# Tokens in rows of five and four: one row layout for q, k, v, the mixers and the output of a linear-attention and phase-mixing kernel

## The chip, the cores and the metric

The kernel runs on one core of a Trainium2 chip. The metric is the device time of one execution in microseconds (us), lower is better. "Before" ran in 232.32 us (median of 3 runs, 231.84 to 232.75). A profile is one further execution taken by the hardware profiler; its span is some 2 us shorter than the time. The engines are PE (matrix multiplication), PEld (its weight load), DVE (vector), ACT (scalar), POOL and SP. SP computes nothing here: it issues the DMA transfers. "SPq" in a profile is SP's sequencer, that is, the time in which SP is occupied with issuing.

## The reference, cut to what matters

```python
# q, k, v: (8 batches, 8 heads, 576 tokens, 64), float32
kv  = einsum('bhsd,bhse->bhde', k, v)
out = einsum('bhsd,bhde->bhse', q, kv)
x   = out / sqrt(mean(out*out, -1) + 1e-6) * g_norm      # -> (8, 576, 512)
theta = x @ w_theta
zr, zi = x * cos(theta), x * sin(theta)
y   = w_tok_r @ zr + w_tok_i @ zi        # "mixers": 576 x 576, over tokens
u   = x + y
return u + maximum(u @ w_ch, 0)
```

576 tokens are four and a half times the 128 rows (partitions) of the core's on-chip memory. The half is the subject of the change. Batches are independent, but theta needs all heads of a batch, and the mix needs all tokens of it.

## The kernel before: the parts that the change touches

A list scheduler in the kernel orders some thousand tasks by estimated times and then emits them; the order on every engine is fixed by it. A token layout puts tokens 0 to 511 into 128 rows of four, and the last 64 tokens ("tails") into tiles of their own:

```python
# load, per head pair: one transfer of 128 rows, two heads, 1 KB each (256 KB)
nc.sync.dma_start(
    out=t[:].rearrange("p h j d -> p h (j d)"),
    in_=src[b, pair, 0:SF, :].rearrange("h (p j) d -> p h (j d)", j=NF))
# batch 0 only, k and v: 128 rows of (head, token row), nine tokens each (288 KB)
    in_=src[b, pair].rearrange("h (p j) d -> (h p) (j d)", j=NS)
# tails, per batch and tensor: 64 rows x 8 heads x 256 B
nc.sync.dma_start(out=t[0:T], in_=src[b, :, SF:S, :].rearrange("h s d -> s h d"))
...
# mixer weights and output: 128 rows per transfer, the tails apart
chunk(name, w[0:SF, :].rearrange("(p j) s -> p j s", j=NF)[:, j, :] if j < NF else w[SF:S, :], ...)
nc.sync.dma_start(out=out[b, 0:SF, :].rearrange("(p j) c -> p j c", j=NF)[:, ti, :], in_=t[:])
for (half, r) in parts:                      # the output's tail: two transfers
    nc.sync.dma_start(out=out[b, SF:S, r * n:(r + 1) * n], in_=t[half])
```

The mixers are cast to fp16 by POOL alone. Batch 0 goes through the attention by head pair (a short chain), batch 1 and later by token tile. While PE has nothing else to do in the first 43 us it runs "warm" products whose results nobody reads.

## Time and profile before

| What | Value | Where read |
|---|---|---|
| time | 232.32 us | runs |
| PE busy, of it warm products | 220.8 us, 23.4 us | busy table, groups |
| first theta product | 25.19 us | timeline |
| batch 1's first theta, batch 1's first mix | 53.79, 68.44 us | timeline |
| from there to the last batch's last block of 63 mix products | 143.7 us, about 24 per batch | timeline |
| from there to the end of the span | 18.2 us | timeline |

These are lines of the page of the profile of before: the engines' busy time, two rows of tenths over 40 equal slices of the span (granted PE clock, DMA share), and the chain of waits that ended last.

```profile
PE 220.8 (96%) x2342; PEld 145.8 (63%) x2342; DVE 185.2 (80%) x368; ACT 157.3 (68%) x298; POOL 88.0 (38%) x108
...
PEclk9999999999999999999999999999999999999999
DMA  5899999999749996974899467996894412103214
...
PE 73%; DMA 9%; DVE 6%; ACT 5%; POOL 3%; issue 1%; SPq 1%; DVEq 0%
PE y L893 27%; PE vps L937 11%; PE th L806 11%; PE kv L524 6%; DMA wst<-in_moe_w_theta_dram 4%; PE xTps L775 4%; PE ups L928 4%; PE warm L293 3%; DMA vl<-in_v_dram 3%; PE raw L572 3%; DMA v<-in_v_dram 2%; POOL rt L594 2%; ACT tr L849 2%; DV
```

The chain is PE's, and SP's own share of it is 1%. DMA counts at the start, where the first batch comes in. PE busy at 96% overstates the bound, because the warm products are in it. The Trainium skill, "Trainium Kernel Development and Optimization", section "Performance Expectations", calls matmul busy time a bad measure for another reason, that matmuls are pipelined. That it misleads here through idle-filling products is this trace's own finding.

The stages of the batches show the bound better. This is a view by windows (columns: from, to and length in us, then busy us of PE, PEld, DVE, ACT, POOL with the number of instructions, granted PE clock, DMA share, GB/s). Two steady batches of before:

```profile
92.40:116.40 24.00, 23.80 (x267) 16.39 (x266) 22.14 (x45) 18.67 (x36) 10.46 (x10) 1.00 0.75 213
116.40:140.40 24.00, 24.00 (x266) 16.35 (x264) 21.53 (x45) 18.00 (x35) 9.94 (x10) 1.00 0.77 224
```

PE is busy in all but 0.2 us of the first window and in all of the second. And this is how SP issues the first loads: the timeline of SP in the first 3 us (start, duration, engine and line, what).

```profile
0.73 0.45 SPq L308 DMA_DIRECT2D q<-in_q_dram  x1
1.24 0.45 SPq L314 DMA_DIRECT2D k<-in_k_dram  x1
1.74 0.43 SPq L314 DMA_DIRECT2D v<-in_v_dram  x1
2.21 0.43 SPq L308 DMA_DIRECT2D q<-in_q_dram  x1
```

One 128-row transfer occupies SP for 0.43 to 0.45 us here.

### The profile page before, as it was taken

The page shows a single profiled execution, that of the slowest core. Times are in us where ns is not written, and L with a number is a line of the kernel's source. Part 1 is how long each engine was busy: PE and PEld are TensorE (multiplying, and loading weights), DVE is VectorE, ACT ScalarE, POOL GpSimd, SP SyncE. Part 2 cuts the span into 40 slices and gives each one's busy share as a digit, 9 for nine tenths or more (in the row PEclk, how much of TensorE's full clock was granted, in tenths as well). Part 3 has the DMA queues.
Part 4 walks back from the last instruction along what each step waited for, and adds up shares of the span by engine and source line. Part 5 has one row for each costly group of instructions (what it writes and reads, how often), then busy time and mean ns, then how long its engine had stood idle before and what let it go on. Part 6 is the DMA issues. An engine that isn't in the chain of part 4 may idle for free.

```text
span 230.3 us, 5955 instructions
## 1 busy us (share of the span) xinstructions
PE 220.8 (96%) x2342; PEld 145.8 (63%) x2342; DVE 185.2 (80%) x368; ACT 157.3 (68%) x298; POOL 88.0 (38%) x108
## 2 busy tenths in 40 slices
PE   7999999999996999999999999999999999999992
PEld 2674555786754665677667766865675668655861
DVE  2268599279997798799999997998799989987553
ACT  2477687327995688767896877589849797877031
POOL 8000197436513670464266033543275336430000
PEclk9999999999999999999999999999999999999999
DMA  5899999999749996974899467996894412103214
GB/s 184 291 344 239 291 254 313 330 272 335 127 124 260 340 162 159 331 235 82 190 317 353 90 151 213 318 195 155 234 306 122 117 57 93 48 23 137 71 46 159
DMA packets 59931, 46.42 MB, mean 202 GB/s; under 512 B 29056, under 2 KB 52608, under 8 KB 59904
## 3 DMA queue, kind: packets, MB, share of 16 engines
q1 hardware_dynamic: 59840, 46.05, 71.9%
q8 instruction: 18, 0.29, 0.6%
q14 instruction: 9, 0.07, 0.1%
q0 software_dynamic: 64, 0.00, 0.0%
HBM read 33.06 MB, written 9.44 MB: 185 GB/s over the span
## 4 chain that ended last, share of the span: by engine, by line
PE 73%; DMA 9%; DVE 6%; ACT 5%; POOL 3%; issue 1%; SPq 1%; DVEq 0%
PE y L893 27%; PE vps L937 11%; PE th L806 11%; PE kv L524 6%; DMA wst<-in_moe_w_theta_dram 4%; PE xTps L775 4%; PE ups L928 4%; PE warm L293 3%; DMA vl<-in_v_dram 3%; PE raw L572 3%; DMA v<-in_v_dram 2%; POOL rt L594 2%; ACT tr L849 2%; DVE x L606 2%; PE wTps L432 2%; PE th L811 1%
## 5 line engine op out<-in xcount | busy, mean ns | idle before, releaser
L893 PE MATMUL y<-wT,z 128*128 128x320 f16 (+1 forms) x576 | 79.1, 286 | 2.2 <-DVE z L859 2.2
L893 PEld LDWEIGHTS <-z 128*128 128x128 f16 x576 | 54.0, 98 | 19.1 <-DVE z L859 2.8
L594 POOL TENSOR_TENSOR rt<-ss,mhalf 128x8 f32<-128x8 f32 x35 | 61.0, 1744 | 2.9
L590 POOL TENSOR_SCALAR ss<-ss 128x8 f32<-128x8 f32 x35 | 9.5, 271 | 85.2 <-DVE ss L583 84.6
L901 DVE SCALAR_TENSOR_TENSOR uT<-y,gcol,xT 128x256 f16<-128x256 f32 (+1 forms) x64 | 32.7, 512 | 7.9 <-PE y L893 7.6
L937 PE MATMUL vps<-wch,uT 128*128 128x512 f16 (+1 forms) x192 | 37.7, 344 | 0.0
L818 ACT ACTIVATE pt<-th,magic_t 128x512 f32<-128x512 f32 (+1 forms) x40 | 25.7, 642 | 16.6 <-PE th L806 13.3
L806 PE MATMUL th<-wth,xT 128*128 128x512 f16 x128 | 32.7, 380 | 0.0
L784 ACT ACTIVATE xT<-xTps,gcol 128x512 f16<-128x512 f16 (+1 forms) x36 | 22.9, 635 | 13.3 <-PE xTps L775 13.0
L944 ACT COPY u<-ups 128x512 f16<-128x512 f16 (+1 forms) x40 | 21.0, 537 | 14.9 <-PE ups L928 14.6
L859 DVE TENSOR_TENSOR z<-x,tr 128x1024 f16<-128x1024 f16 (+1 forms) x40 | 27.0, 674 | 3.4 <-ACT tr L849 1.7
L948 DVE SCALAR_TENSOR_TENSOR ot<-vps,u 128x512 f32<-128x512 f32 (+1 forms) x40 | 25.2, 633 | 4.1 <-PE vps L937 2.6
L822 DVE SCALAR_TENSOR_TENSOR f<-pt,th 128x512 f32<-128x512 f32 (+1 forms) x40 | 25.2, 629 | 4.0 <-ACT pt L818 3.7
L606 DVE TENSOR_TENSOR x<-raw,rt 128x512 f16<-128x512 f32 x36 | 24.7, 685 | 3.0 <-POOL rt L594 2.4
L583 DVE TENSOR_REDUCE ss<-sq 128x8 f32<-128x512 f32 x36 | 24.3, 680 | 2.3 <-ACT sq L579 2.0
L293 PE MATMUL warm<-kvbd 128*128 128x512 f16 x81 | 23.4, 410 | 2.0 <-DVE pio_t L250 1.5
L841 ACT ACTIVATE tr<-fa,pio_t 128x512 f16<-128x512 f32 x32 | 23.0, 720 | 0.5 <-DVE fa L829 0.3
L841 ACT ACTIVATE tr<-f 128x512 f16<-128x512 f32 x32 | 20.2, 630 | 3.4 <-DVE f L822 3.2
L579 ACT ACTIVATE sq<-raw 128x512 f32<-128x512 f32 x36 | 21.1, 591 | 1.2 <-PE raw L572 0.9
L937 PEld LDWEIGHTS <-uT 128*128 128x128 f16 (+1 forms) x192 | 14.1, 102 | 8.1 <-issue 0.4
L524 PE MATMUL kv<-v,k 128*64 128x64 f32 x448 | 19.0, 227 | 0.0
L524 PEld LDWEIGHTS kv<-v,k 128*64 128x64 f32 x448 | 15.3, 137 | 5.6 <-issue 4.2
(80 smaller groups left out, 243.4 us busy)
## 6 DMA issues: line engine op xcount, KB each, us to landing
q<-in_q_dram SPq DMA_DIRECT2D x32, 256.0 KB, 5.1
out_dram<-ot SPq DMA_DIRECT2D x32, 256.0 KB, 3.6
k<-in_k_dram SPq DMA_DIRECT2D x28, 256.0 KB, 5.1
v<-in_v_dram SPq DMA_DIRECT2D x28, 256.0 KB, 5.5
k<-in_k_dram SPq DMA_DIRECT2D x4, 288.0 KB, 6.2
v<-in_v_dram SPq DMA_DIRECT2D x4, 288.0 KB, 6.4
wmix<-in_moe_w_tok_r_dram SPq DMA_DIRECT2D x4, 288.0 KB, 5.5
wmix<-in_moe_w_tok_i_dram SPq DMA_DIRECT2D x4, 288.0 KB, 4.0
```

Source lines behind the costliest of these rows:

```text
L293: nc.tensor.matmul(t[:], kv_bd[1][:, 0, :], kv_bd[1][:].rearrange("p h c -> p (h c)"), start=True, stop=True,)
L524: nc.tensor.matmul(kvp[r * D:(r + 1) * D, hp, :], st["k", b, hp][:, r, j, :] if j < NF else st["kl", b][:, 2 * hp + r, :], st["v", b, hp][ ...
L594: nc.gpsimd.tensor_tensor(out=r[:], in0=t[:], in1=mhalf[:], op=ALU.pow)
L606: nc.vector.tensor_tensor(out=t[:].rearrange("p (h e) -> p h e", h=H), in0=st[raw][:].rearrange("p (h e) -> p h e", h=H), in1=st[rt][:].un ...
L806: nc.tensor.matmul(t[:], xT[:, kc, :], wth[:, kc, :], start=(kc == 0), stop=(kc == NK - 1),)
L818: nc.scalar.activation(out=t[:], in_=st[th][:], func=AFT.Identity, bias=magic_t[:])
L822: nc.vector.scalar_tensor_tensor(out=t[:], in0=st[pt][:], scalar=MAGIC, in1=st[th][:], op0=ALU.subtract, op1=ALU.subtract,)
L841: nc.scalar.activation(out=t[:, which, :], in_=src[:], func=AFT.Sin, scale=-RAD, bias=0.0 if bias is None else bias[:],)
L859: nc.vector.tensor_tensor(out=t[:], in0=xb.unsqueeze(1).broadcast_to((P, w, C)), in1=st[tr][:, 0:w, :], op=ALU.mult,)
L893: nc.tensor.matmul(t[:], z[:, kc * P:(kc + 1) * P], wT[m][:, cols], start=(m == 0), stop=(m == NM - 1),)
L901: nc.vector.scalar_tensor_tensor(out=st["uT", b][:, kc, cols], in0=st[y][:], scalar=gcol[:], in1=st["xT", b][:, kc, cols], op0=ALU.mult, o ...
L937: nc.tensor.matmul(t[half], uT(kc), wch[:, kc, r * n:(r + 1) * n], start=(kc == 0), stop=(kc == NK - 1),)
```

## The change

Its intent: no separate tails (no tail loads, no tail casts, fewer products in batch 0), and a shorter start. The 576 tokens are laid in 128 rows of which 64 hold five tokens and 64 hold four: rows 0 to 63 take tokens 0 to 319, rows 64 to 127 tokens 320 to 575. The fifth slot of the lower rows is the tail. As five and four do not fit one regular access pattern, each load becomes two transfers of 64 rows; so do the mixers' loads and the stores. Besides, batch 1 goes by head pair like batch 0, the mixers are cast whole by whichever of POOL, DVE and ACT is free, they are loaded before batch 1, batch 0's mix adds up as its tiles arrive, the evictions of the first half of a mix merge two chunks, g_norm is brought into a column by a small product, and the scheduler's target times are new. The core of the diff:

```diff
-                    nc.sync.dma_start(
-                        out=t[:].rearrange("p h j d -> p h (j d)"),
-                        in_=src[b, pair, 0:SF, :].rearrange("h (p j) d -> p h (j d)", j=NF),
-                    )
+                for (rows, tokens, n) in ((slice(0, T), slice(0, L0), NT), (slice(T, P), slice(L0, S), NF)):
+                    nc.sync.dma_start(
+                        out=t[rows, :, 0:n, :].rearrange("p h j d -> p h (j d)"),
+                        in_=src[b, 2 * hp:2 * hp + 2, tokens, :].rearrange("h (p j) d -> p h (j d)", j=n),
+                    )
... (the tails' loads, casts and tiles go)
-                chunk(name, w[0:SF, :].rearrange("(p j) s -> p j s", j=NF)[:, j, :] if j < NF
-                      else w[SF:S, :], mixers + 0.1 + 0.1 * i + 0.01 * j)
+                parts = [(slice(0, T), lower(w)[:, j, :])]
+                if j < NF:
+                    parts.append((slice(T, P), upper(w)[:, j, :]))
+                chunk(name, parts, mixers + 0.1 + 0.1 * i + 0.01 * j)
-            weave.add(name, on[2:] if pool else on[:2], at, fn, needs=[of], uses=[of])
+            weave.add(name, [act(n), dve(0.06 + n / 1900.0, True), pool(n)], at, fn,
+                      needs=[of], uses=[of])
...
-                nc.sync.dma_start(
-                    out=out[b, 0:SF, :].rearrange("(p j) c -> p j c", j=NF)[:, ti, :], in_=t[:]
-                )
+                nc.sync.dma_start(out=lower(out[b])[:, ti, :], in_=t[0:T])
+                nc.sync.dma_start(out=upper(out[b])[:, ti, :], in_=t[T:P])
                 return
-            for (half, r) in parts:
-                nc.sync.dma_start(out=out[b, SF:S, r * n:(r + 1) * n], in_=t[half])
+            nc.sync.dma_start(
+                out=lower(out[b])[:, NF, :].rearrange("t (r c) -> r t c", r=len(parts)), in_=t[:]
+            )
+    SP2 = ("SP", 0.15, 0.15, False)     # the scheduler's cost of two transfers, us
```

## The prediction

> **What bounds the kernel.** TensorE. The page's busy table gives PE 220.8 of 230.3 us (96%), DVE 185.2, ACT 157.3; the chain of waits is 73% PE. But the groups by line show 81 idle-filling "warm" matmuls (23.4 us) in that PE time, so real PE work is about 197 us. By stage:
>
> - 0 to 25 us: PE waits. The timeline shows 51 warm matmuls (spaced 0.22 us, about 11 us) before the first theta product at 25.2 us. The chain there is DMA: v, w_theta (3.8% of the span), v tails (3.1%). Batch 0's last v is used at 16.1 us; the chain from there to turned x takes 8 us, then PE stands behind batch 1's k/v tails.
> - 25 to 68 us: mixed. 30 more warm matmuls (6.5 us), because the mixer weights are cast by POOL alone from 28.2 to 38.6 us; mix of batch 0 starts at 44.3, theta of batch 1 at 53.8, mix of batch 1 at 68.4 with PE idle 2.7 us in 60 to 80 us.
> - 68 to 212 us: PE saturated, 24.0 us per batch (six mix starts); a batch's PE groups sum to about 23.7.
> - 212 to 230 us: the last mix and channel product, 18 us.
>
> **What the change does.**
>
> 1. Tails as fifth slot: the 22 tail loads (512 packets of 256 B each, landing 4 us) and 8 tail casts (3.3 us DVE) go; batch 0's kv takes 10 instead of 18 slot pairs (about 0.85 instead of 1.2 us per pair of heads). Against it every q/k/v load is two DMAs of 64 rows, 24 issues of about 0.4 us for batch 0, and the instruction order shows that each DMA waits for the one eight before it, so half as many bytes are in flight. The Trainium skill, "SBUF — State Buffer", section "Door 1: The DMA port swizzle", says 64 adjacent rows reach half of the 16 ports; no run shows yet whether this bites.
> 2. Batch 1 goes by head pair: its theta follows its last pair by one short chain.
> 3. Mixers are cast whole by POOL, DVE and ACT, loaded before batch 1.
> 4. Batch 0's mix opens its sums as z tiles come; first-half mix evictions merge two chunks (DVE about 15 us falls to an estimated 10).
> 5. Mixer transposes double in number (45 to 90) but pair up on half the columns: estimated +1 us at most. Warm matmuls fall 81 to 39.
>
> **On the critical path.** What comes before mix of batch 1. Batch 0's 3.54 MB plus 1.05 MB at an estimated 325 GB/s land at about 14 and 17 us; with a 7 us chain theta starts near 21.5 us (gain 3.7). PE work from there to batch 1's theta sums to about 27 us, plus 9 warm: near 50 (gain 4). Mix of batch 1 near 63 instead of 68.4. The rest, 144 + 18 us, is PE-bound and equal: the evictions' saving on DVE is off the path.
>
> **Predicted: 225.0 us, 221.5 to 228.5 in 8 of 10.** Faster by over 2% 0.80, within 2% 0.18, slower 0.02.
>
> **What would show it.** First theta at 20 to 23 us; wT complete and batch 0's mix begun near 30; batch 1's theta at 47 to 51; mix starts 24 us apart after 63; last 18 us unchanged; warm time about 9 us; loads landing in 3 to 4 us at 300 GB/s or more.
>
> **What would make it wrong.** Half-port or half-depth loads falling under 280 GB/s early; ACT's order (a mixer cast ahead of batch 0's last turn) making theta wait for the mixers; new PE stalls from z or PSUM banks in the steady batches, so that the early gain is given back.

## The result

The changed kernel is correct and took 280.66 us (median of 4 runs, 279.3 to 282.49) against 232.38 us (median of 4, 231.84 to 232.75). The ratio is 1.2085, with a 95% interval of 1.2008 to 1.2162. Ratios here and below are the mean time of one kernel's fast runs over the mean of the other's fast runs of the same rounds, so not quite the ratio of the medians that are quoted. The predicted 225.0 us and its range were missed by far, in the wrong direction.

The same lines of the page, after, with PE's own row of busy tenths as well:

```profile
PE 230.3 (82%) x2283; PEld 152.7 (54%) x2283; DVE 184.5 (66%) x369; ACT 156.9 (56%) x299; POOL 76.7 (27%) x92
...
PE   7669929998798597697957799859967999999980
PEclk9876975999999799889997599979997999999998
DMA  5779868987767776777577666677466723403333
...
PE 36%; DMA 24%; SPq 20%; DVE 9%; issue 4%; POOL 2%; ACT 1%; POOLq 1%; DVEq 0%; ACTq 0%
PE y L864 13%; SPq L327 12%; DMA qin<-in_q_dram 12%; DMA out_dram<-ot 8%; PE vps L920 6%; PE kv L484 4%; PE th L768 4%; SPq L347 3%; SPq L467 3%; DVE x L554 2%; DMA wst<-in_moe_w_theta_dram 2%; DMA vin<-in_v_dram 2%; PE ups L911 2%; DVE ot 
```

DVE and ACT do as much as before. PE's share of the chain fell from 73% to 36%, and SP's sequencer went from 1% to 20%: L327 is the issue of the 64-row q, k and v. The DMA share is lower than before in 20 of the 40 slices and higher in 11, and over the span the hardware queue's packets took 64.2% in place of 71.9%: on the whole the DMA engines are not overloaded, they are waiting for work. The granted clock fell in places. The two rows above show its low digits (5 to 7) in slices where PE's own digit is 7 or less, or in the slice right after one (the 5 in the seventh slice follows PE's 2), so I take it as a companion of the waiting and use no slow-clock argument below. It is not free, though: PE was busy for 230.3 us here, and for 210.4 us with the same 2283 instructions in a2 below, at a clock of 0.916 against 0.991. How much of the loss passed through the clock no run separates.

SP in the timeline of after, at the start and where w_theta, the mixers and batch 1 are issued (x2 is two transfers):

```profile
0.73 1.44 SPq L327 DMA_DIRECT2D qin<-in_q_dram  x2
2.21 1.26 SPq L327 DMA_DIRECT2D kin<-in_k_dram  x2
...
16.52 3.02 SPq L347 DMA_DIRECT2D wst<-in_moe_w_theta_dram  x4
19.59 0.51 SPq L347 DMA_DIRECT2D wmix<-in_moe_w_tok_r_dram  x1
...
32.39 1.29 SPq L327 DMA_DIRECT2D qin<-in_q_dram  x2
```

A 64-row transfer occupies SP for 0.6 us and comes 0.65 us after the one before it. The first two pairs, when nothing else is queued yet, are no faster (1.44 and 1.26 us for two). So batch 0's 24 issues end at 16.5 us, where before had issued w_theta's first piece at 8.65; then come w_theta and the mixers' 18 transfers, and batch 1's loads start at 32.4 us. A steady batch looks no better. SP's timeline from 92.6 us on:

```profile
92.59 0.55 SPq L938 DMA_DIRECT2D out_dram<-ot  x1
93.18 0.59 SPq L939 DMA_DIRECT2D out_dram<-ot  x1
93.82 1.35 SPq L327 DMA_DIRECT2D qin<-in_q_dram  x2
95.27 1.24 SPq L327 DMA_DIRECT2D kin<-in_k_dram  x2
96.55 1.25 SPq L327 DMA_DIRECT2D vin<-in_v_dram  x2
...
102.64 7.21 SPq L467 DMA_TRANSPOSE qT<-qcast  x5
```

The sum for one batch is an estimate from these durations: 24 loads at 0.65, 9 stores at 0.6 and 5 transposing transfers at 1.27 us make 15.6 + 5.4 + 6.4 = 27.4 us of SP alone, more than the 24.0 us that PE needs. In before the same kind of sum gives an estimate of about 17 us. SP's timeline, added up, confirms it: between the first mix products of batches 1 and 5 of after (83.3 to 212.9 us) SP was issuing for 117.8 us, with gaps of under 0.12 us for 9.1 more, so for 98% of 129.6 us; the limit of eight transfers in flight, which the prediction names, cannot have held it back there for more than the rest. In before the same stretch (68.4 to 165.6 us) gives 82%. Nor were the DMA engines full there: their share in after was 0.64 to 0.73, at 168 to 185 GB/s. The chain of waits of after, in order of time, shows it as a row of nothing but issues:

```profile
141.82 0.61 SPq L327
142.43 0.04 issue
142.48 0.60 SPq L327
143.08 0.04 issue
143.13 0.61 SPq L327
...
147.77 7.03 DMA out_dram<-ot
```

The last of these lines is a store that was issued after these loads and landed 7 us later.

To see where the 50.4 us of span came from, I cut every kernel at three marks that all traces have: batch 1's first mix product, the start of the last batch's closing block of mix products, the end. For before they lie at 68.44, 212.10 and 230.3 us, for after at 83.28, 257.90 and 280.7.

| Kernel (profile) | first theta | start: to batch 1's mix | steady: to the last block | end |
|---|---|---|---|---|
| before | 25.19 | 68.4 | 143.7 | 18.2 |
| after | 27.99 | 83.3 | 174.6 | 22.8 |
| difference | +2.8 | +14.8 | +31.0 | +4.6 |

So there are three losses, the largest in the steady batches, where I had predicted none.

### The profile page after: what moved, and what is told of

Its sections match the earlier page's. It is cut to its first block, busy times and chain, and to the rows that moved or that the text cites. A ratio compares the mean times of both kernels' runs of the same rounds, so it can differ in the third digit from the quotient of the medians.

```text
span 280.7 us, 6020 instructions
## 1 busy us (share of the span) xinstructions
PE 230.3 (82%) x2283; PEld 152.7 (54%) x2283; DVE 184.5 (66%) x369; ACT 156.9 (56%) x299; POOL 76.7 (27%) x92
## 3 DMA queue, kind: packets, MB, share of 16 engines
q1 hardware_dynamic: 51184, 46.06, 64.2%
## 4 chain that ended last, share of the span: by engine, by line
PE 36%; DMA 24%; SPq 20%; DVE 9%; issue 4%; POOL 2%; ACT 1%; POOLq 1%; DVEq 0%; ACTq 0%
PE y L864 13%; SPq L327 12%; DMA qin<-in_q_dram 12%; DMA out_dram<-ot 8%; PE vps L920 6%; PE kv L484 4%; PE th L768 4%; SPq L347 3%; SPq L467 3%; DVE x L554 2%; DMA wst<-in_moe_w_theta_dram 2%; DMA vin<-in_v_dram 2%; PE ups L911 2%; DVE ot L931 2%; DVE qcast L454 2%
## 5 line engine op out<-in xcount | busy, mean ns | idle before, releaser
L864 PE MATMUL y<-wT,z 128*128 128x320 f16 (+1 forms) x576 | 86.3, 306 | 0.7 <-DVE uT L875 0.6
L864 PEld LDWEIGHTS <-z 128*128 128x128 f16 x576 | 58.4, 105 | 19.6 <-issue 1.7
L542 POOL TENSOR_TENSOR rt<-ss,mhalf 128x8 f32<-128x8 f32 x31 | 51.9, 1675 | 2.6
L484 PE MATMUL kv<-vin,kin 128*64 128x64 f32 x640 | 27.3, 237 | 17.4 <-DMA vin<-in_v_dram 17.3
L931 DVE SCALAR_TENSOR_TENSOR ot<-vps,u 128x512 f32<-128x512 f32 (+1 forms) x40 | 25.3, 635 | 22.8 <-DMA out_dram<-ot 18.8
L484 PEld LDWEIGHTS kv<-vin,kin 128*64 128x64 f32 x640 | 23.4, 147 | 24.2 <-issue 20.2
L875 DVE SCALAR_TENSOR_TENSOR uT<-y,gcol,xT 128x320 f16<-128x320 f32 (+1 forms) x48 | 29.3, 613 | 9.6 <-PE y L864 9.6
L454 DVE CAST qcast<-qin 128x640 f16<-128x640 f32 x32 | 15.7, 491 | 29.2 <-DMA qin<-in_q_dram 29.2
L821 DVE TENSOR_TENSOR z<-x,tr 128x1024 f16<-128x1024 f16 (+1 forms) x32 | 19.8, 619 | 3.2 <-ACT tr L811 1.9
L531 DVE TENSOR_REDUCE ss<-sq 128x8 f32<-128x512 f32 x32 | 21.1, 679 | 0.6 <-ACT sq L527 0.6
L768 PEld LDWEIGHTS <-xT 128*128 128x128 f16 x128 | 11.9, 101 | 16.2 <-issue 5.1
```

The source lines that it names most:

```text
L484: nc.tensor.matmul(kvp[r * D:(r + 1) * D, hp, :], st["k", b, hp][:, r, j, :], st["v", b, hp][:, r, j, :], start=(j == 0), stop=(j == NT - 1),)
L542: nc.gpsimd.tensor_tensor(out=r[:], in0=t[:], in1=mhalf[:], op=ALU.pow)
L768: nc.tensor.matmul(t[:], xT[:, kc, :], wth[:, kc, :], start=(kc == 0), stop=(kc == NK - 1),)
L864: nc.tensor.matmul(st[y][:, c, :], z[:, kc * P:(kc + 1) * P], wT[m][:, cols], start=(c == 0 and m == 0) if open_sums else m == 0, stop=m = ...
L875: nc.vector.scalar_tensor_tensor(out=st["uT", b][:, chunks, cols], in0=st[y][:], scalar=gcol[:], in1=st["xT", b][:, chunks, cols], op0=ALU ...
L931: nc.vector.scalar_tensor_tensor(out=t[:], in0=st[vp][:], scalar=0.0, in1=st[u][:], op0=ALU.max, op1=ALU.add,)
```

## The experiments

Two causes were open for the loads. Theory I: SP's issue of 64-row transfers (0.6 us each). Theory P: 64 adjacent rows reach only half of the memory ports. The Trainium skill, "SBUF — State Buffer", section "Door 1: The DMA port swizzle", says that rows 0 to 63 cover 8 of 16 ports and lists 196 GB/s for them (1 MiB transfers) against 328 for all 128 rows; its section "Can I just issue two DMAs to hit both halves?" answers no. (The expectation of m1 puts both statements under the first of these sections.) A third theory, W, was that the number of transfers in flight or simply their count does it. Twelve kernels ran.

### m1: a kernel of transfers alone

Only transfers, in stretches of one form each, with a wait for all of them in between:

```diff
+    for n in range(12):                      # and so on for the other forms
+        for half in (0, 1):
+            nc.sync.dma_start(out=room(n, 2, half), in_=part(n, 2, half))
+    gap()
```

> A kernel that only issues DMAs from the SP queue, in groups with one shape each, and writes zeros (wrong on purpose). Theory I (a DMA of 64 rows holds the SP queue for about 0.61 us, one of 128 rows for 0.33 to 0.47 us, whatever its bytes): 64-row DMAs of 4 and 8 heads hold the queue as long as those of 2 heads, and their group moves 290 KB per 0.65 us or more, over 300 GB/s. Theory P (64 rows reach half of the 16 ports, and two such DMAs do not overlap: the Trainium skill, SBUF - State Buffer, Door 1): every group of 64-row DMAs stays at 196 to 220 GB/s however large the DMA, and landing times grow with the size. Theory W (eight DMAs in flight, of half the bytes): 24 DMAs of 128 rows and 128 KB each are as slow per byte as the 64-row ones, about 225 GB/s.

The groups of SP's issues in this kernel (minimum, median and maximum ns of one). L78 is 128 rows of two heads, L82, L86 and L90 are 64-row halves of two, four and eight heads, L93 is 128 rows of one head, L118 is 96 rows:

```profile
L82 SPq DMA_DIRECT2D big<-in_q_dram x24: 601/605/722, 29.7 to 44.8; - x24
L86 SPq DMA_DIRECT2D big<-in_q_dram x24: 595/596/616, 48.3 to 71.1; - x24
L93 SPq DMA_DIRECT2D big<-in_q_dram x24: 340/430/432, 117.0 to 128.1; - x24
...
L78 SPq DMA_DIRECT2D big<-in_q_dram x12: 367/469/619, 16.9 to 23.3; - x12
...
L90 SPq DMA_DIRECT2D big<-in_q_dram x12: 595/2417/2757, 81.8 to 100.7; - x12
...
L118 SPq DMA_DIRECT2D big<-in_q_dram x12: 312/448/450, 225.8 to 231.3; - x12
```

And the same stretches by window (length, DVE, POOL, PE clock, DMA share, GB/s), in the order 128 rows, 64 rows of two, four and eight heads, and further down 128 rows of eight heads:

```profile
16.88:29.73 12.85, 0.67 (x2) 0.00 (x0) 1.00 0.75 245
29.73:48.27 18.54, 0.18 (x1) 0.00 (x0) 1.00 0.65 191
48.27:81.78 33.51, 0.18 (x1) 0.00 (x0) 1.00 1.01 211
81.78:117.00 35.22, 0.18 (x1) 0.00 (x0) 1.00 1.02 201
...
174.06:194.94 20.88, 0.18 (x1) 0.00 (x0) 1.00 0.94 301
```

A 64-row transfer of two or four heads costs 0.6 us of issue whatever its bytes, and a 128-row transfer of one or two heads 0.43 to 0.47. With eight heads the least is 0.6 us as well, but the median is 2.4 us: there SP is held up. With larger 64-row transfers the issue is no longer the limit, the DMA share goes to 1.0, and the rate still stays at 201 to 211 GB/s, where 128 rows reach 301. So theory I's "over 300 GB/s" failed, and P's 196 to 220 GB/s came out for the larger transfers. Theory W got something too: 128-row transfers of one head averaged 224 GB/s in their stretch (117.0 to 131.1 us), about what it had named, though above the 191 of 64-row ones of the same number. Both costs are real; which of them binds where has to be asked of the kernel.

### b1 and b2: the kernel before with its loads cut in two

b1 cuts every q, k and v load of before into two of 64 rows; b2 cuts it by head into two of 128 rows. Both are correct, and the order of all computing is that of before.

```diff
 b1
+                    for r in range(2):
                         nc.sync.dma_start(
-                        out=t[:].rearrange("p h j d -> p h (j d)"),
+                            out=t[r * PH:(r + 1) * PH].rearrange("p h j d -> p h (j d)"),
 b2
+                            out=t[:, r].rearrange("p j d -> p (j d)"),
```

> The kernel before, with each q, k, v load cut in two DMAs of 64 rows; every other instruction in the same order; right result. I and P both: SP needs about 27 us per batch where 24 are there, so 250 to 265 us. W: the same slowdown as b2_split_heads. S (the new order of work is at fault, not the DMAs): 232 to 236 us.

> The kernel before, with each q, k, v load cut in two DMAs of 128 rows, one head each (batch 0's k and v: 5 and 4 of 9 tokens); as many DMAs and bytes per DMA as b1_split_rows. I: issues of 0.33 to 0.4 us each, about 21 us per batch, still under 24: 232 to 238 us. P: 232 to 236 us. W: as slow as b1_split_rows.

b1 took 274.22 us (273.27 to 275.42, ratio 1.1814, 1.1767 to 1.1861), b2 246.67 us (245.07 to 248.22, ratio 1.0624, 1.0566 to 1.0682); before was at 232.19. So the 64-row cut alone, without anything else of the change, makes 42 of the 48 us (and 9 us more than the expected 265). In the traces of b1 and b2 the issues of q take 616 and 430 ns (median), as in m1. b1's marks are 81.2, 172.6 and 18.3 us, so its steady loss is 28.9 us where that of after is 31.0; b2's are 73.2, 151.8 and 18.3. W falls as the main cause, because b2 makes as many transfers as b1. But b2 lies over 8 us above the ranges of I and P: twice as many 128-row transfers cost 14 us. The traces show why, and it is theory I again with a better sum: over the four batches from batch 1's first mix product on, SP was issuing (short gaps included) for 99% of 104.7 us in b2, 25.8 us per batch where about 21 had been estimated, and for 98% of 122.1 us in b1.

### a1 and a2: the changed kernel with whole transfers

a1 loads each q, k and v of a head pair by one 128-row transfer of the same bytes. The tokens land in wrong places, so the result is wrong, but order, sizes and number of all computing instructions are those of after. a2 also loads the mixers and stores the main tiles in 128 rows.

```diff
 a1
-                for (rows, tokens, n) in (...lower..., ...upper...):
-                    nc.sync.dma_start(out=t[rows, :, 0:n, :]..., in_=src[b, 2 * hp:2 * hp + 2, tokens, :]...)
+                nc.sync.dma_start(
+                    out=t[:].rearrange("p h j d -> p h (j d)")[:, :, 0:S * D // P],
+                    in_=src[b, 2 * hp:2 * hp + 2].rearrange("h s d -> h (s d)").rearrange(
+                        "h (p x) -> p h x", p=P))
 a2, in addition
+                parts = [(slice(0, P), w[0:SF].rearrange("(p j) c -> p j c", j=NF)[:, j, :])
+                         if j < NF else (slice(0, T), w[SF:S, :])]
```

> The changed kernel with each q, k, v tile loaded by one DMA of 128 rows, the same bytes in one shape (4.5 tokens per row: wrong result on purpose), order of all compute engines unchanged. I, P and W: SP falls to about 18 us per batch, and the time to 225 to 235 us. S: stays over 270 us.

> a1_loads_whole with the mixers' chunks and the stores in one DMA of 128 rows each as well (wrong result on purpose; compute engines' orders unchanged): no 64-row DMA is left but the two mixer tails. In a1 the 18 mixer DMAs held the SP queue for 13 us, batch 1's first v was issued at 27.4 us and TensorE stood still from 27.9 to 31.0 us. If that took the gain that was predicted: batch 1's first v is issued near 22 us, mix of batch 1 starts near 65 us instead of 69.5, and the time is 225 to 229 us. If the order of work itself gives nothing: 231 to 234 us, as a1.

a1 took 232.43 us (230.84 to 233.44, ratio 1.0011, 0.9950 to 1.0073), a2 225.53 us (225.3 to 225.69, ratio 0.9732, 0.9696 to 0.9768; before at 231.88). Both lie in the expected ranges, and a2's batch 1 mix starts at 65.1 us as expected. The halves of the loads cost 48 us and those of mixers and stores 7 us more; with whole transfers the rest of the change costs nothing net. The page of a2 and its chain of waits:

```profile
PE 210.4 (94%) x2283; PEld 142.5 (64%) x2283; DVE 182.1 (81%) x369; ACT 155.7 (70%) x299; POOL 76.8 (34%) x92
...
PEclk9999999999999999999999999999999999999996
...
PE 63%; DMA 11%; DVE 10%; POOL 6%; SPq 3%; ACT 2%; issue 2%; POOLq 1%
```

PE is the bound again. Its first theta starts at 21.57 us, batch 1's at 51.84 us. a2 is no usable kernel, but it prices what the change would be worth with whole transfers: 6.4 us.

### f1: two head pairs per 64-row transfer

Half as many 64-row transfers, each of twice the bytes. f1 is correct. Its buffers are three double ones in place of six, and the scheduler's order moved.

```diff
-    "k": 6, "v": 6, "q": 6, ...
+    "k": 3, "v": 3, "q": 3, ...          # tiles of four heads
-                        in_=src[b, 2 * hp:2 * hp + 2, tokens, :].rearrange(
+                        in_=src[b, 2 * hp:2 * hp + 4, tokens, :].rearrange(
```

> The changed kernel with q, k, v of two head pairs in one 64-row DMA pair: half as many load DMAs with twice the bytes, still 64 rows; right result; the list scheduler gives another order. Theory I alone (issues): SP has 12 loads of 0.65, 9 stores of 0.6 and 5 transposes of 1.27 us per batch, 19.6 us where 24 are there: 228 to 240 us. Theory P (half of the ports, 205 to 215 GB/s in m1_issue for 64-row DMAs of these sizes): 4.7 MB of loads and stores per batch take 22 to 23 us of the DMA engines, and the transposes come on top: 250 to 268 us, with landing times of 5 us and more.

The three fast runs took 264.36 to 265.68 us (ratio 1.1435, 1.1386 to 1.1484). A fourth was at 363.45 us with a granted clock of 0.563, and the profile is of that run, so I read no stage from it. Halving the issues bought 15 us, half of the 31 us that the steady part had lost. That fits the range stated for P and lies far above the 228 to 240 us of I alone, but the coarser buffers and the other order are mixed in, and no fast profile shows the stage.

### c1, c2, c3: everything but the row layout

c1 keeps all of the change except the layout: rows and tails as before. c2 is c1 with the scheduler's steady target times of before and the output's tail stored by two transfers. c3 is c2 with the tails read as 64 packets of 2 KB in place of 512 of 256 B. Its output is wrong, which doesn't matter for the time.

```diff
 c1
+                    in_=src[b, pair, 0:SF, :].rearrange("h (p j) d -> p h (j d)", j=NF)   # and the tails
 c2
-    "load": (-23.01, 4.21),
+    "load": (-15.33, 2.93),                 # from batch 2 on; cast, norm, ... likewise
 c3
-                    out=t[0:T], in_=src[b, :, SF:S, :].rearrange("h s d -> s h d")
+                    in_=src[b, 0, 0:SF, :].rearrange("(p j) d -> p (j d)", j=H),
```

> The changed kernel with the rows as before (128 rows of 4 tokens, tails apart, 128-row DMAs) and all else of the change kept: batch 1 by head pair, mixers cast whole on three engines and loaded before batch 1, merged first-half evictions, open sums, g_norm turned by TensorE. Right result. If the 64-row DMAs are all that is wrong with the change: 224 to 230 us, faster than both kernels. If not: 231 us or more.

> A candidate to beat both, correct: c1 (all of the change except the row layout, so whole 128-row loads and separate tails) with the times at which the list scheduler wants the steady stages taken from the kernel before (loads 8 us later, casts, norm and attention later), and the tail of the output stored by two transfers. If c1 lost its early gain because the steady schedule was tuned for the other layout (SP stood behind stores with loads behind it, q landed 7.6 us after its issue), the mix starts from batch 2 on come 24 us apart and the time is 223 to 229 us. If the loss comes from the tails' packets or from batch 1 by head pairs with separate tails, it stays at 235 us or more.

> c2 with one thing changed, wrong on purpose: the tails of q, k and v are read as 64 rows of 2 KB (64 packets) from other tokens instead of 64 x 8 packets of 256 B. Bytes, number of transfers, compute order and layout are those of c2. If the small packets of the separate tails hold up the loads behind them (in c2 the DMA engines are 92 to 109% busy up to 100 us at 209 to 284 GB/s, PE waits for v at 85 to 100 us and idles 3.3 us in 80 to 100 us), the time falls to 226 to 232 us, and the change's first part (no separate tails) was worth about 8 us by itself. If the loss of c1 and c2 comes from elsewhere (the 18 slot pairs of batch 0, the schedule), it stays at 236 us or more.

c1 took 239.52 us (238.65 to 240.02, ratio 1.0333, 1.0294 to 1.0371), c2 238.42 us (236.63 to 239.38, ratio 1.0241, 1.0143 to 1.0339; before at 232.47). c3's two fast runs took 235.12 and 238.13 us, two more 239.7 and 240.75 (the ratio, 1.0323, 1.0250 to 1.0396, fits the mean of the three slowest; the two fast ones are 2.1% above the mean of before, whose median was 231.88). The hopes of c1 (224 to 230 us), c2 and c3 all failed: neither the target times nor the size of the tails' packets accounts for the loss. Batch 1's mix starts at 67.4 us in c2, 1 us earlier than in before, and at 63.4 in c3, so the larger packets did shorten the start; but the steady part takes 149.4 us in c2 and 150.0 in c3 in place of 143.7, and the end 20.0 and 19.9 in place of 18.2. (In c1 it is 146.7 and 23.7.) Against a2's 137.3 this suggests that the parts of the change lean on each other: without the tails in the fifth slot the rest does not pay. By c1's own test, the 64-row transfers are then not all that keeps a correct form of the change from gaining. Why the steady part of c1 to c3 is long I could not settle. In none of the three is it the 64-row issue of the main loads, which is gone: SP was issuing for 76 to 77% of the four batches in c2 and c3. No candidate here beats before.

### m2: who issues, and which rows

A second kernel of transfers alone, to part I from P:

```diff
+    def pair_of_halves(n, first, second):
+        first.dma_start(out=room(n, 2, 0), in_=part(n, 2, 0))
+        second.dma_start(out=room(n, 2, 1), in_=part(n, 2, 1))
+    # SP and SP; SP and ACT; SP and POOL; every second row; 128 rows of one head as [64, 2, 320]; ...
```

> A kernel of DMAs alone, wrong on purpose, with a stretch for each way of loading the same 3.5 MB of q as 64-row transfers. It separates two causes that the first microbenchmark found together: the 0.6 us that SP needs to issue one 64-row transfer (I) and the about 200 to 215 GB/s that 64 adjacent partitions reach (P). Stretch 1, lower and upper halves both from SP: as before, about 0.6 us each and 190 GB/s. Stretch 2, lower halves from SP, upper halves from ACT's queue: if I binds and both halves together reach all ports, 0.65 us per pair and about 270 GB/s or more; if P binds, at most about 215 GB/s. Stretch 3, upper halves from POOL's queue: the same question, with POOL's own issue cost unknown, I expect about 1 us each. Stretch 4, 64 rows on every second partition, SP alone: if the cost of the issue comes from the 64 rows, 0.6 us each and about 190 GB/s again; if it comes from adjacency of partitions, 0.35 to 0.45 us and above 250 GB/s. Stretch 5, 128 overlapping rows of five tokens, one head each: 0.43 us, about 250 GB/s or more. Stretch 6, whole 128-row pairs alternating between SP and ACT: above 245 GB/s if SP's issues were the limit of the whole pairs, 245 if not. Stretches 7 and 8, 48 and 80 rows: issue cost by rows, 0.45 to 0.6 us. Last, the tail store of the changed kernel as one transfer [2, 64, 256] against two [64, 256]: landing 5 us or more against about 2 to 3 us.

By window, in this order: both halves from SP, SP and ACT, SP and POOL, 64 rows on every second partition, 128 rows as [64, 2, 320].

```profile
16.89:35.08 18.19, 0.48 (x1) 0.00 (x0) 1.00 0.67 195
35.30:51.68 16.38, 0.00 (x0) 0.00 (x0) 1.00 0.81 216
51.90:68.17 16.27, 0.00 (x0) 7.09 (x12) 1.00 0.82 218
68.38:87.28 18.90, 0.00 (x0) 0.00 (x0) 1.00 0.64 188
87.50:104.69 17.19, 0.00 (x0) 0.00 (x0) 1.00 0.79 229
```

And the issues of the last two forms, and of 48 (L108) and 80 rows (L111):

```profile
L93 SPq DMA_DIRECT2D big<-in_q_dram x24: 602/604/621, 68.4 to 84.3; - x24
L100 SPq DMA_DIRECT2D big<-in_q_dram x24: 548/604/606, 87.5 to 102.4; - x24
...
L108 SPq DMA_DIRECT2D big<-in_q_dram x12: 338/425/430, 117.0 to 122.1; - x12
L111 SPq DMA_DIRECT2D big<-in_q_dram x12: 313/442/444, 126.8 to 132.0; - x12
```

SP, ACT and POOL all need about 0.6 us for one (for POOL 1 us had been expected). SP and POOL together issue all 24 in 8.1 us where SP alone takes 15.7, and SP and ACT start at that pace too but then pause, yet the rate rises only from 195 to 218 or 216 GB/s. So the second issuer gains 11 to 12%, and the skill's "no" to the two-halves question holds here; the 6% that the page gives compares two transfers at once with one. Whole pairs, alternating between SP and ACT, reached 260 GB/s (104.9 to 117.0 us) where SP alone had 245 in m1. The 0.6 us is not a matter of adjacent rows, because every second row costs it too, nor of the number of rows alone, because 48, 80 and 96 rows cost 0.43 to 0.45; both were expected otherwise. It came with every load of q whose outer dimension was 64, even with 128 rows written as [64, 2] (229 GB/s, where 250 or more had been expected). The change's tail store, with an outer dimension of 2, takes 0.57 us as well. Why, no run shows. In the last stretches the tail store of the change as one transfer of [2, 64, 256] moved 48 GB/s, two of [64, 256] 94.

### e1: the changed kernel with the upper halves issued by POOL

One expression of after is changed; it is correct, and bytes and layout stay.

```diff
-                    nc.sync.dma_start(
+                    (nc.sync if n == NT else nc.gpsimd).dma_start(
```

> The changed kernel, correct, with only the issuer of the upper halves of q, k and v changed from SP to POOL; compute order, bytes and layout stay. The DMA microbenchmark gave 0.65 us per pair of halves when both queues issue, but still only 217 GB/s. Theory I (SP's issues at 0.6 us each bound the steady batches: 27.4 us of SP per batch against 24.0 of PE): SP falls by 12 x 0.65 to about 19.6 us per batch, so from the third batch on mix starts come 24 to 26 us apart, and the kernel ends between 237 and 252 us. Theory P (the steady batches are bound by what 64-row transfers reach): 3.54 MB per batch at 217 GB/s are 16.3 us, already under 24, but if landing still binds, mix starts stay 30 us or more apart and the time above 260. Both agree on the start: the 3.54 MB of batch 0 take 16.3 us by either limit, so the first theta product stays at 26 to 29 us, 5 us or more later than with whole loads. A cost of its own: POOL is busy 12 x 0.6 us more per batch and may delay the powers of the norm.

e1 took 255.64 us (255.1 to 258.0, ratio 1.1016, 1.0927 to 1.1105; before at 232.47), 25 us less than after. The mark table says where:

| Kernel (profile) | first theta | start: to batch 1's mix | steady: to the last block | end |
|---|---|---|---|---|
| before | 25.2 | 68.4 | 143.7 | 18.2 |
| after | 28.0 | 83.3 | 174.6 | 22.8 |
| e1, upper halves from POOL | 25.7 | 83.7 | 147.5 | 22.8 |
| a1, loads whole | 21.1 | 69.5 | 137.8 | 22.9 |
| a2, all whole | 21.6 | 65.1 | 137.3 | 21.5 |

The steady part fell by 27.1 us, to 24.6 us per batch: it was SP's issue time, and taking 12 of the 24 issues off SP cures most of it. Over four batches SP was issuing for 85% of the time, where it had been 98%. (The mean spacing of 24.0 us from the third batch on, though single ones reach 26.7, and the first theta are inside the expectation; the total is 3.6 us above it.) The start stays at 83.7 us although SP has half as many loads to issue. These are two windows of e1 up to the first mix of batch 0:

```profile
0.00:25.70 25.70, 19.50 (x177) 10.42 (x178) 14.40 (x47) 10.06 (x25) 12.57 (x30) 0.93 0.92 231
25.70:47.90 22.20, 13.99 (x133) 8.37 (x132) 11.84 (x26) 11.59 (x23) 8.90 (x14) 0.69 1.01 249
```

The DMA share is 0.92 and 1.01 at 231 and 249 GB/s: by that share the engines are full, and what 64-row transfers reach is the likely limit. In a2 the slices of about the same time carry 301 (0 to 20 us) and 338 GB/s (20 to 40 us) by the view by windows, and in a1, whose mixers are halves as in e1, 285 (0 to 21 us) and 294 (21 to 38.5 us). So both theories hold, each in its stage: I in the steady batches, which e1 shows; P at the start, which e1 supports (more issuers do not shorten it) together with a1 (whole rows do, by 14 us). In after itself SP was issuing for 45.4 of the first 48.3 us, short gaps included, at DMA shares of only 0.76 and 0.80: by these figures SP's limit came first there and the rate's close behind. That issuing from POOL has a cost of its own at the start was not ruled out. POOL paid for it: its busy time rose from 76.7 to 135.0 us, and DVE waits for POOL's powers for 7.1 us in e1, which may be part of the distance from 147.5 to a1's 137.8; I did not test that.

### a3: the tail store

a2 with the tail of the output stored by two transfers, as in before. Its output is wrong, which doesn't matter for the time.

```diff
-            nc.sync.dma_start(out=out[b, SF:S, :].rearrange("t (r c) -> r t c", r=len(parts)), in_=t[:])
+            for (half, r) in parts:
+                nc.sync.dma_start(out=out[b, SF:S, r * n:(r + 1) * n], in_=t[half])
```

> a2 (all loads and stores whole, wrong on purpose) with the tail of each batch's output stored by two transfers of [64, 256] as the kernel before does it, instead of one of [2, 64, 256]. In a2 the last tail store lands 6 to 7 us after its issue and ends the span; the microbenchmark moved 48 GB/s with the one transfer and 94 with two. Expected 3 to 4 us less than a2's 225.5: 221 to 223 us. If the last store's form costs nothing, 225 again. This prices the change's tail store apart from its loads.

Two runs took 222.68 and 222.72 us at a clock of 1.0, two 227.03 and 227.56 at 0.974 to 0.985 (ratio of the fast ones 0.9598, 0.9534 to 0.9661; before at 231.88). The fast pair is 2.8 us below a2, inside the expected 221 to 223 us; the profile is of a slow run, but its end part, 225.2 less the mark at 206.40, is 18.8 us where a2's is 21.5, so the gain sits where it should. The Trainium skill, "DMA: Bandwidth & Descriptors", section "Why a DMA increments its semaphore by 16 and not by 1", says that the number of DMA engines that a transfer uses must divide the outermost dimension that isn't 1, on both sides. An outer dimension of 2 allows two. The measured 48 against 94 GB/s agree in direction, and in m2's stretch of such stores the DMA share was 0.14 of 16 engines, which is about two.

## Why the prediction was wrong

The step that failed is the first: "Against it every q/k/v load is two DMAs of 64 rows, 24 issues of about 0.4 us for batch 0". A 64-row issue takes 0.6 us at a spacing of 0.65. The 0.4 us came from before's 128-row transfers; but before's own trace had 64-row transfers, the tail loads, at 595 to 766 ns each, which I had taken for the cost of their many small packets. (In c3, with 64 packets in place of 512, they still take 517 to 595 ns, medians by tensor.) And the sum was drawn for batch 0 alone. Had it been drawn for a steady batch, with the stores and the transposing transfers, the result would have been 27.4 us of SP against 24.0 of PE.

Point by point:

- That PE bounds the kernel: right for before and again for a2. For after it is wrong; SP's queue took its place in the steady batches (98% issuing; e1 shows that it was the limit).
- "Batch 0's 3.54 MB plus 1.05 MB at an estimated 325 GB/s land at about 14 and 17 us": wrong. The page of before shows 184 to 344 GB/s in its first ten slices. The last of batch 0 is only issued at 16.5 us. The two limits happen to be close: one pair of halves, 288 KB, every 1.3 us is 227 GB/s, and with two issuers a whole stretch still averages only 216 to 218 (m2). First theta came at 27.99 us in place of 21.5. With whole transfers (a2) it came at 21.57.
- The half-port warning: I had cited it and left it open, and listed "half-port or half-depth loads falling under 280 GB/s early" among what would make the prediction wrong. It was right to list it, and wrong to give it almost no weight: slower had a chance of 0.02.
- Batch 1's theta "near 50", its mix "near 63 instead of 68.4": 66.65 and 83.3 in after; 51.84 and 65.1 in a2. With whole transfers (a2) the mechanism (head pairs, mixers cast by three engines and loaded first) came out as said, 2 us too hopeful.
- "The rest, 144 + 18 us, is PE-bound and equal": wrong in after (174.6 and 22.8). In a2 both terms were mis-sized as well, with opposite signs: the steady part was 137.3 us, 6.4 less than before, and the end 21.5, 3.3 more, of which a3 puts 2.7 down to the tail store. So a2's 225.53 us beside the predicted 225.0 confirms the picture in the large, but partly because errors cancel.
- "Warm matmuls fall 81 to 39": that is the number in after. Their value in the sum did not matter.

What stays open: why an outer dimension of 64 makes an issue dear, how much of the start is the rate's and how much SP's, and why c1 to c3 lose 3 to 6 us in the steady batches and 2 to 6 at the end. No correct layout with whole transfers was run, so a2's 225 us remain a price and no kernel.

## What to carry to other kernels

Draw up the time budget of the queue that issues the transfers, per steady iteration, as for a compute engine: number of transfers of each shape times the issue time of that shape, read from a trace, against the time of the bounding engine. A layout that is tidier for the computing but turns 128-row transfers into 64-row ones pays twice, in issue time (0.65 in place of 0.5 us, and twice as many) and in rate (in the kernels of transfers alone, 64-row loads averaged at most 218 GB/s, 128-row ones 224 to 301). More transfers of 128 rows pay in issue time too: b2 lost 14 us. When a change moves work onto an engine that was 1% of the chain, that engine needs the closest costing.

## What the Trainium skill lacked or had wrong

- "DMA: Bandwidth & Descriptors" gives about 50 ns for the dispatch of a transfer by its sequencer, in the list of its path from POOL, and no issue time by the shape of a transfer on this chip. Here the issuing engine is occupied for 430 to 469 ns with a 128-row load of one or two heads from SP (medians, m1), for 425 to 448 with 48, 80 or 96 rows, and for 594 to 610 with 64 rows of two or four heads or an outer dimension of 64; ACT and POOL needed as long as SP for the 64-row halves (m1, m2).
- The same page, section "Issuing engines are not separate DMA queues", says that issuing from several engines only saves sequencer time, "which is usually small relative to the DMA itself". The first half agrees with m2 (from 195 to at most 218 GB/s). The second, taken as a rule, misleads for a kernel whose transfers are many: taking 12 of 24 load issues per batch off SP saved 25 us of 281 (e1).
- "SBUF — State Buffer", "Door 1: The DMA port swizzle", is roughly borne out and not wrong here: 182 to 211 GB/s for 64 rows of q in m1, 301 for 128 rows. The page's answer on two halves holds as well: a second issuer gained 11 to 12% (m2).
